# A sparse-attention and spectral-mixing kernel: its last two modes by column halves, the first output item's identity products moved, and four-mode weight transfers from an earlier pair on

## The chip, the cores and the metric

The kernel runs on one core of a Trainium2 chip. The metric is the device time in microseconds (us); the runs of the kernel before have a median of 425.84. The core has a matrix engine (PE, with its weight loads listed as PEld), a vector engine (DVE), an activation engine (ACT), a general engine (POOL) and a sync engine (SP). Sixteen DMA engines move data; POOL and SP issue the transfers here. PE writes its results into PSUM, which has 8 banks of 2 KB in each of 128 partitions; ACT and DVE read them from there.

## The reference

Attention over 8 batches, 8 heads, 576 positions and 64 channels, with a local mask for the first four heads and a strided one for the others; then a spectral layer over the 576 positions with 64 modes, each with its own complex 512 x 512 weight, and a residual product with `w_ch`.

```
scores = scale * np.matmul(q, k.transpose(0, 1, 3, 2))
mask_local = (rel >= 0) & (rel < stride)                    # heads 0 to 3, stride 32
mask_strided = (rel >= 0) & (pos[None, :] % stride == pos[:, None] % stride)
attn = softmax(np.where(masks, scores, -1e9));  x = np.matmul(attn, v)   # to (8, 576, 512)
X = np.fft.rfft(x, axis=1)[:, :n_modes]
Yr = np.einsum('bmd,mde->bme', Xr, w_r) - np.einsum('bmd,mde->bme', Xi, w_i)
Yi = np.einsum('bmd,mde->bme', Xr, w_i) + np.einsum('bmd,mde->bme', Xi, w_r)
y = np.fft.irfft(Yr + 1j * Yi, n=S, axis=1)
u = x + y
return u + np.maximum(u @ w_ch, 0.0)
```

The weights `w_r` and `w_i` are 64 x 512 x 512 in float32, 134 MB together; everything else is small beside them.

## The kernel before

**Weights.** A mode's weights are worked in two halves of the 512 input rows, so there are 128 half-modes, listed in `ORDER` (L150) in the order of their use. Two neighbours make a pair, 64 pairs in all. `w_fetch` (L161) issues the transfers from POOL, one for `w_r` and one for `w_i`, with a cast to float16. Most go into `wring`, a ring of five pair buffers; pairs 1, 2 and 7 (`GUEST`) go into tiles that are needed for something else later. `w_fetch` counts freed pair buffers; it issues the next transfer when there are enough: one for a pair, two if the pair's number is in `QUADS` (L153), in which case one transfer brings four half-modes (this pair and the next). The first eight pairs are fetched during the strided attention; after that each `mode_pair` (L589) calls `w_fetch` when its pair has been multiplied, unless that pair was in a guest tile. Three of the `w_r` transfers (those that begin at half-mode 64, 84 and 94) are cut by `UNEVEN` into pieces of uneven row counts (L187). The last four half-modes come one by one (L194). POOL also issues the loads of q, k and v (`load_str`, `load_loc`); `load_loc` for batch 6 is the last one before the local attention starts, and the one for batch 7 follows after the first 14 half-modes.

**Stages.** Strided attention, then local attention with the first 56 half-modes between its steps, then 48 half-modes of the other half with the "premix" products `x @ w_ch`, then the `rest` (L1061): 8 half-modes of slot 0 and 16 of slot 1, with the inverse transforms of the first 48 modes (`renew`) hung between them by the table `late`. All instructions stand in program order (`manual_schedule`): each engine works its own queue in that order and waits by semaphores.

**PSUM in the last stage.** A pool `p` with three double banks (`psum("p", pair=True)`) and a pool `y` with two banks. A new tile takes the next buffer of its pool in turn, and its first writer waits until the old tile's readers are done. Slot 0's modes and slot 1's first 48 go through `mode_pair`; slot 1's modes from 48 on are worked by `mode` (L618) itself: 16 products of 128 x 128 weights by 16 columns each, four per block `e` of 128 output channels; eight modes share one `y` tile. `spectrum` (L563) then moves finished modes to SBUF: DVE adds them to what slot 0 left, giving the tile `YT`. In the last group modes 56 to 61 are moved together and then 62 and 63 together (`ends`, L643).

**The end.** The 18 output items (`items`) are pairs of 128-row blocks. Item k has two sums, v and u, each in a double bank: `v_early` (L994) and `u_early` (L1002) start them with two identity products each; `new_rows` (L1009) adds the inverse transform of the last 16 modes, from `zzs` (for v) and `yys` (for u); `v_done` (L1036) is ACT's relu of v, `u_done` (L1048) is DVE's sum and SP's transfer to the output. `u_early` takes its buffer from `p` for even items and from `u` for odd ones. For the first four batches `zzs[0]` comes from `spec_z(3, 0, ...)` (four products with `w_ch`, L745) and `yys[0]`, `yys[1]` from eight transposes (L1076). Before the change these two steps use a pool of their own (`ps_s`) in the space of `y`, and `u` is opened in that space afterwards. The hook `late[22]` runs between modes 62 and 63.

Of the kernel before, what the change touches and what calls it, by code (L numbers as in the profile page):

```python
# [10 lines left out]
FP = mybir.dt.float32  # L11
F16 = mybir.dt.float16
# [7 lines left out]
NM = 64  # L20
# [36 lines left out]
def kernel(  # L57
# [10 lines left out]
    nc = tc.nc  # L68
    PSUM = bass.MemoryType.PSUM
# [5 lines left out]
    pss = {}  # L75
# [10 lines left out]
    def psum(kind, half=False, pair=False):  # L86
        if pair:
            return pss[kind].tile([128, 2, 512], FP, tag=kind, name=kind)
        if half:
            return pss[kind].tile([128, 1024], F16, tag=kind, name=kind)  # L90
        return pss[kind].tile([128, 512], FP, tag=kind, name=kind)
# [19 lines left out]
    idn = cs["cI"]  # L111
# [8 lines left out]
    YS = {}  # L120
# [29 lines left out]
    ORDER = [(1, m) for m in range(SPLIT1)] + [(0, m) for m in range(SPLIT0)]  # L150
    ORDER += [(1, m) for m in range(SPLIT1, NM)] + [(0, m) for m in range(SPLIT0, NM)]
    UNEVEN = {64: (25, 12, 27), 84: (6, 54, 4), 94: (10, 54)}
    QUADS = {p for p in range(13, 54) if (p - 13) % 5 in (0, 2)}  # L153
    wring = pw.tile([128, 2 * NWBUF, 4, DM], F16, tag="w", bufs=1, name="wring")
    w_tiles = []
    w_chs = {}
# [4 lines left out]
    def w_fetch(n=1):  # L161
        free_pairs[0] += n
        while len(w_tiles) < 2 * NM:
            i = len(w_tiles)
            pair = i // 2
            nm = 4 if pair in QUADS else 2
            if 2 * free_pairs[0] < nm:
# [86 lines left out]
    def act_copy(out, in_):  # L254
        nc.scalar.activation(out=out, in_=in_, func=ACTF.Copy)  # L255
# [300 lines left out]
    ypt = {}  # L556
    queued = []

    def flush():
        while queued:  # L560
            queued.pop()()

    def spectrum(slot, part, src):  # L563
        if slot == 0:
            nc.scalar.activation(out=YS["Y0"][part], in_=src, func=ACTF.Copy)
        else:
            nc.vector.tensor_tensor(
                out=YS["YT"][part], in0=src, in1=YS["Y0"][part], op=AluOp.add
            )
# [19 lines left out]
    def mode_pair(slot, m):  # L589
        half = 1 - slot  # L590
        if m % 4 == 0:
            ypt[slot] = psum("y")
        yp = ypt[slot]
        steps = [(c, mm) for c in range(4) for mm in (m, m + 1)]
        if m == 0:
            steps.sort(key=lambda x: x[1])
        for c, mm in steps:
            wt = w_tiles[ORDER.index((half, mm))]
            pr = ds(0, 128 if mm else 64)
            a = 32 * (mm % 4)  # L600
            nc.tensor.matmul(  # L601
                yp[ds(a, 32), :],
                Xh[half][pr, c].rearrange("p b r (h m) -> p (b r h) m", h=2)[
                    :, :, mm % 32
                ],
                wt[pr, XC[c], :],
                start=(c == 0),
                stop=(c == 3),
                tile_position=(0, a),
            )  # L610
        if slot or m // 2 not in GUEST:
            w_fetch()
        if m % 4:
            yr = big.tile([128, DM], F16, tag="yr", name="yr")
            act_copy(yr, yp)
            queued.append(lambda: four_turned(slot, m - 2, yr))

    def mode(slot, m):  # L618
        half = 1 - slot
        if m % 2:  # L620
            flush()
        if slot == 0 or m < SPLIT0:
            if m % 2:
                mode_pair(slot, m - 1)
            return
        mi, mg = m % 8, m // 8
        if mi == 0:
            ypt[slot] = psum("y")
        yp = ypt[slot]
        yv = yp.rearrange("p (m e x) -> p m e x", m=8, e=4)  # L630
        wt = w_tiles[ORDER.index((half, m))]
        for e in range(4):
            for c in range(4):
                nc.tensor.matmul(
                    yv[:, mi, e, :],
                    wt[:, XC[c], ds(128 * e, 128)],
                    Xh[half][:, c, :, :, m],
                    start=(c == 0),
                    stop=(c == 3),
                )  # L640
        if m % 2:
            w_fetch()
        ends = {5: 6, 7: 2} if mg == 7 else {7: 8}  # L643
        if mi in ends:
            n = ends[mi]
            m0 = mi + 1 - n
            spectrum(
                slot,
                (slice(None), slice(None), mg // 2, slice(None), ds(8 * (mg % 2) + m0, n)),
                yp.rearrange("p (m e x) -> p e x m", m=8, e=4)[:, :, :, ds(m0, n)],  # L650
            )
# [90 lines left out]
    def spec_z(g, bq, zp):  # L742
        for e in range(4):
            lhs = YS["YT"][:, e, g, ds(8 * bq, 8), :].rearrange("p x m -> p (x m)")
            nc.tensor.matmul(  # L745
                zp, lhs, w_chs["n"][:, e, :], start=(e == 0), stop=(e == 3)
            )
# [102 lines left out]
    for b in range(B):  # L850
# [3 lines left out]
        ends = [lambda h=h: loc_scores(b, h, True) for h in (0, 2)]  # L854
# [23 lines left out]
    zzs = [ptr.tile([128, DM], F16, name=f"zz{i}") for i in range(B)]  # L878
    yys = [ptr.tile([128, DM], F16, name=f"yy{i}") for i in range(B)]
# [22 lines left out]
    for b in range(B + 1):  # L902
        for t in range(5):
            if b > 0 and (t < 4 or b % 2 == 0):
                work.append(lambda b=b, t=t: premix(b - 1, t))
            if b < B and t < 4:
                half, cp = ((1, 0), (1, 1), (0, 0), (0, 1))[t]
# [68 lines left out]
    late = {0: [lambda: spec_late(spec_z, zzs, act_copy)], 1: [spec_last]}  # L976
    for n, i in enumerate([3, 5, 7] + list(range(8, 21))):
        b, t = n // 2, n % 2 * 2
# [15 lines left out]
    def v_early(k):  # L994
        vps[k] = psum("p", pair=True)
        for j, r in enumerate(own(items[k], v0s, v0h)):
            nc.tensor.matmul(vps[k][:, j], idn, r, start=True, stop=False)  # L997

    def pooled(k, j):
        return j == 1 and k in (4, 5, 6)  # L1000

    def u_early(k):  # L1002
        ups[k] = psum(("p", "u")[k % 2], pair=True)
        for j, r in enumerate(own(items[k], xos, xoh)):
            if pooled(k, j):
                continue
            nc.tensor.matmul(ups[k][:, j], idn, r, start=True, stop=False)
# [51 lines left out]

    flush()  # L1060
    rest = [(0, m) for m in range(SPLIT1, NM)] + [(1, m) for m in range(SPLIT0, NM)]  # L1061
    late[22] = [lambda: v_early(0), lambda: v_early(1), lambda: u_early(0)]
    for i, (slot, m) in enumerate(rest):
        mode(slot, m)
        for w in late.get(i, ()):
            w()
    yctx.close()
    with tc.tile_pool(name="ps_s", bufs=1, space=PSUM) as pss["s"]:
        zp = pss["s"].tile([128, 512], FP, name="zp")
        yp = pss["s"].tile([128, 2, 512], F16, name="yp")  # L1070
        spec_z(3, 0, zp)
        act_copy(zzs[0], zp)
        for bq in range(2):
            for e in range(4):
                lhs = YS["YT"][:, e, 3, ds(8 * bq, 8), :].rearrange("p x m -> p (x m)")
                nc.tensor.transpose(yp[:, bq, ds(128 * e, 128)], lhs, idn)  # L1076
        for bq in range(2):
            nc.vector.tensor_copy(out=yys[bq], in_=yp[:, bq])
    pss["u"] = pctx.enter_context(tc.tile_pool(name="ps_u", bufs=1, space=PSUM))

    for k in range(2):
# [1 line left out]
    for k in range(2):  # L1083
        v_done(k)
    for k in range(2):
        if k:
            u_early(k)
        new_rows(k, ups[k], yys)
        u_done(k)
    for k in range(2, LAST + 2):  # L1090
# [47 lines left out]
```

## Time and profile before

| | us |
|---|---|
| median of 3 runs (425.5 to 427.29) | 425.84 |
| profiled execution | 425.88 |
| its span, first to last instruction | 424.1 |
| PE busy | 340.9 (80%) |
| DVE busy | 234.6 (55%) |
| ACT busy | 219.0 (52%) |
| POOL busy | 95.7 (23%) |
| first output transfer issued (SP) | 395.42 |
| last output transfer issued (SP) | 419.1 |

A busy share is an average over the whole span, and the stages differ: what sets the time has to be read stage by stage. Matmuls overlap in the profile, so PE's share is not its share of peak. The granted clock of PE was 0.933 on average. The profile names an engine's idle time by what ended it ("<-DMA wring" is a wait for a weight transfer, "<-PE y" one for a product). The trace also stamps each transfer's completion once for each of the sixteen DMA engines; a reader of the data waits for the last of them.

The transfers by size, from the list of DMA issues: 17 of `w_r` and 16 of `w_i` have 1024 KB (four half-modes), 22 and 24 have 512 KB (pairs), and three of each in the guest tiles have 512 KB. The outputs are 14 transfers of 512 KB and 8 of 256 KB.

### The profile page before, as it was taken

How to read it: one execution, taken by the hardware profiler on the slowest of the kernel's cores; microseconds unless marked ns; L12 is line 12 of the kernel's file. 1: busy time of each engine (PE TensorE's matmuls, PEld its weight loads, DVE VectorE, ACT ScalarE, POOL GpSimd, SP SyncE). 2: the span in 40 equal slices, each digit the busy share in tenths (PEclk: the TensorE clock that was granted, in tenths of full speed). 3: DMA queues.
4: the chain of work that ended last, by engine and by line, in shares of the span. 5: the costliest groups of instructions: out<-in, count | busy, mean ns of one | idle time of the engine just before them, and what ended most of it. 6: DMA issues, size and time to landing. Idle time of an engine off the chain costs nothing.

```text
span 424.1 us, 9718 instructions
## 1 busy us (share of the span) xinstructions
PE 340.9 (80%) x4164; PEld 206.5 (49%) x4164; DVE 234.6 (55%) x469; ACT 219.0 (52%) x391; POOL 95.7 (23%) x165
## 2 busy tenths in 40 slices
PE   2987878769999298889874959895779979989993
PEld 2866767554656155556542425453344534535331
DVE  3788788950354134545323326864385646555794
ACT  1687678642666056565753323622162365534772
POOL 7332333322422011102122101212111232310200
PEclk9999899967999789999998789999798998989999
DMA  8999999999999999999999999999999999997598
GB/s 147 211 212 213 213 212 214 210 212 210 214 214 211 215 216 213 214 215 214 211 215 213 212 211 216 213 213 214 213 214 211 214 214 214 213 213 145 196 380 316
DMA packets 30347, 91.62 MB, mean 216 GB/s; under 512 B 3873, under 2 KB 4641, under 8 KB 30305
## 3 DMA queue, kind: packets, MB, share of 16 engines
q0 software_dynamic: 24624, 81.28, 96.7%
q1 hardware_dynamic: 5248, 9.65, 6.2%
q8 instruction: 32, 0.52, 0.5%
q10 hardware_dynamic: 432, 0.08, 0.1%
q14 instruction: 11, 0.08, 0.0%
HBM read 162.83 MB, written 9.44 MB: 406 GB/s over the span
## 4 chain that ended last, share of the span: by engine, by line
PE 46%; DMA 23%; DVE 17%; ACT 8%; issue 4%; POOL 1%; DVEq 0%; ACTq 0%; POOLq 0%
DMA wring<-in_moe_w_i_dram 22%; PE y L601 11%; PE sc L726 5%; DVE xb L245 3%; ACT X L255 3%; DVE kz L287 3%; DVE yy L761 2%; PE p L997 2%; PE tp L417 2%; PE y L536 2%; PE sc L536 2%; PE sc L463 2%; PE p L769 2%; PE p L1018 1%; ACT PL L493 1%
## 5 line engine op out<-in xcount | busy, mean ns | idle before, releaser
L601 PE MATMUL y<-wring,X 128*32 128x512 f16 (+1 forms) x424 | 65.8, 422 | 23.6 <-DMA wring<-in_moe_w_i_dram 23.6
L190 POOL DMA_DIRECT2D wring<-in_moe_w_r_dram x39 | 23.6, 606 | 204.3 <-PE y L601 180.6
L601 PEld LDWEIGHTS <-X 128*32 128x32 f16 (+1 forms) x448 | 27.5, 139 | 41.4 <-DMA wring<-in_moe_w_i_dram 24.3
L735 ACT ACTIVATE v<-sc 128x512 f16<-128x512 f32 x32 | 19.1, 597 | 45.4 <-PE sc L726 45.4
L736 DVE COPY xo<-tp 128x512 f16<-128x512 f16 x32 | 22.1, 691 | 36.5 <-PE tp L734 36.4
L255 ACT ACTIVATE yr<-y 128x512 f16<-128x512 f32 x28 | 16.7, 597 | 41.2 <-PE y L601 41.0
L726 PE MATMUL sc<-w_cp,xT 128*128 128x512 f16 x128 | 36.2, 404 | 1.9 <-DVE xT L694 1.9
L245 DVE TENSOR_TENSOR xb<-av,rec 90x256 f16<-90x256 f32 (+2 forms) x80 | 36.0, 450 | 2.8
L493 ACT ACTIVATE PL<-sc 128x480 f16<-128x480 f32 (+1 forms) x48 | 26.9, 578 | 20.1 <-PE sc L479 19.8
L244 DVE RECIPROCAL rec<-av 90x4 f32<-90x4 f32 (+2 forms) x80 | 14.6, 183 | 39.3 <-PE av L508 28.2
L424 DVE COPY qT<-tp 128x576 f16<-128x576 f16 x16 | 11.9, 752 | 38.1 <-PE tp L417 38.1
L971 DVE TENSOR_TENSOR xo<-p,xo 128x1024 f16<-128x1024 f32 x16 | 19.6, 1225 | 14.3 <-PE p L769 14.3
L190 POOL DMA_DIRECT2D wring<-in_moe_w_i_dram x42 | 25.6, 609 | 6.1 <-DMA ring<-in_k_dram 2.0
L382 ACT ACTIVATE PL<-sc 90x360 f16<-90x360 f32 (+1 forms) x48 | 22.7, 490 | 7.1 <-PE sc L375 6.6
L255 ACT ACTIVATE v<-p 128x1024 f16<-128x1024 f32 x16 | 16.4, 1024 | 17.4 <-PE p L769 17.4
L255 ACT ACTIVATE v<-tp 128x640 f16<-128x640 f16 (+1 forms) x24 | 19.0, 807 | 11.6 <-PE tp L451 9.3
L417 PE MATMUL tp<-cI_s,ring 64*64 64x64 f16 x864 | 22.2, 196 | 2.7 <-DVE qT L424 2.4
L463 PE MATMUL sc<-cMl_s,cI_s 128*128 128x480 f16 (+1 forms) x48 | 18.9, 395 | 5.1 <-ACT PL L493 3.5
L280 PE MATMUL tp<-cI_s,ring 72*128 72x72 f16 x256 | 15.4, 207 | 9.1 <-DMA ring<-in_v_dram 7.4
L255 ACT ACTIVATE kz<-tp 64x360 f16<-64x360 f16 (+1 forms) x32 | 18.9, 592 | 6.2 <-PE tp L417 5.2
L417 PEld LDWEIGHTS <-ring 64*64 64x64 f16 x864 | 17.3, 109 | 9.0 <-issue 4.9
L536 PEld LDWEIGHTS <-xb 108*128 108x128 f16 (+2 forms) x176 | 15.4, 106 | 11.7 <-DVE xb L245 7.6
(146 smaller groups left out, 747.9 us busy)
## 6 DMA issues: line engine op xcount, KB each, us to landing
wring<-in_moe_w_r_dram POOLq DMA_DIRECT2D x17, 1024.0 KB, 13.3
wring<-in_moe_w_i_dram POOLq DMA_DIRECT2D x16, 1024.0 KB, 17.5
wring<-in_moe_w_i_dram POOLq DMA_DIRECT2D x24, 512.0 KB, 15.1
wring<-in_moe_w_r_dram POOLq DMA_DIRECT2D x22, 512.0 KB, 13.4
out_dram<-osb SPq DMA_DIRECT2D x14, 512.0 KB, 3.8
ring<-in_v_dram POOLq DMA_DIRECT2D x8, 288.0 KB, 13.3
ring<-in_q_dram POOLq DMA_DIRECT2D x8, 288.0 KB, 13.5
ring<-in_k_dram POOLq DMA_DIRECT2D x8, 288.0 KB, 13.1
```

Of the source, the lines that this page charges most:

```text
L190: nc.gpsimd.dma_start(dst, rows)
L245: nc.vector.tensor_tensor(out=dst, in0=val.rearrange("p h (q c) -> p h c q", c=4), in1=rec[0:n, 0:pieces] .to_broadcast((n, pieces, 64)) . ...
L255: nc.scalar.activation(out=out, in_=in_, func=ACTF.Copy)
L382: nc.scalar.activation(out=PS[0:n, ds(POFF[t], 4 * n)], in_=scp[0:n, 0 : 4 * n], func=ACTF.Exp, scale=SCALE,)
L417: nc.tensor.transpose(tp[ds(64 * hp, 64), ds(64 * i, 64)], qn[ds(64 * hp, 64), ds(64 * (9 * g + i), 64)], idn[ds(64 * hp, 64), ds(64 * hp, ...
L463: nc.tensor.matmul(scp[:, 0 : n * times].rearrange("p (h x) -> p h x", h=times), idn, mask_rows("cMl", n, times), start=True, stop=False,)
L493: nc.scalar.activation(out=dst, in_=src, func=ACTF.Exp, scale=SCALE)
L536: nc.tensor.matmul(xp[:, ds(192 * cp, 192)].rearrange("p (f m) -> p f m", f=3), xb[b][0:n, base + t, ds(128 * cp, 128)], F[0:n, :, t, :], ...
L601: nc.tensor.matmul(yp[ds(a, 32), :], Xh[half][pr, c].rearrange("p b r (h m) -> p (b r h) m", h=2)[:, :, mm % 32], wt[pr, XC[c], :], start= ...
L726: nc.tensor.matmul(vp, xT[:, ch], w_chs["cp"][:, ch, :], start=(ch == 0), stop=(ch == 3),)
L736: nc.vector.tensor_copy(out=xo.rearrange("p (h q c) -> p h q c", h=2, c=4), in_=tp[:, 0:512].rearrange("p (h c q) -> p h q c", h=2, c=4),)
L971: nc.vector.tensor_tensor(out=xo, in0=up[:, 0:n], in1=xo, op=AluOp.add)
```

## The change

Three parts.

1. `QUADS` starts at pair 8 instead of 13, in the same rhythm: it gains the pairs 8 and 10, so that pairs 8 and 9 come by one transfer of `w_r` and one of `w_i`, and pairs 10 and 11 as well.
2. The last two modes (62 and 63 of slot 1) are written to two new `y` tiles, one for the blocks e = 0, 1 and one for e = 2, 3, instead of the group's tile. In mode 63 each half of both modes is moved by `spectrum` as soon as its two blocks are done.
3. Between modes 62 and 63 only item 1's v is started (two products). Item 0's v is started after the last `spec_z`, ahead of the transposes, and item 0's u just before its `new_rows`. The tiles for `spec_z` and the transposes are taken from `y`; the pool `ps_s` is gone, and `y` is closed after them.

```
-    QUADS = {p for p in range(13, 54) if (p - 13) % 5 in (0, 2)}
+    QUADS = {p for p in range(8, 54) if (p - 8) % 5 in (0, 2)}
...
+        if m == NM - 2:
+            ypt["last"] = [psum("y") for _ in range(2)]
+        if m >= NM - 2:
+            yl = [y.rearrange("p (m e x) -> p m e x", m=8, e=4) for y in ypt["last"]]
         wt = w_tiles[ORDER.index((half, m))]
         for e in range(4):
+            if m >= NM - 2:
+                yv = yl[e // 2]
             for c in range(4):
...
+            if m == NM - 1 and e % 2:
+                es = slice(e - 1, e + 1)
+                spectrum(
+                    slot,
+                    (slice(None), es, mg // 2, slice(None), ds(14, 2)),
+                    yv[:, ds(6, 2), es].rearrange("p m e x -> p e x m"),
+                )
...
-        ends = {5: 6, 7: 2} if mg == 7 else {7: 8}
+        ends = {5: 6} if mg == 7 else {7: 8}
...
-    late[22] = [lambda: v_early(0), lambda: v_early(1), lambda: u_early(0)]
+    late[22] = [lambda: v_early(1)]
     for i, (slot, m) in enumerate(rest):
         mode(slot, m)
         for w in late.get(i, ()):
             w()
+    zp = psum("y")
+    yp = psum("y", half=True).rearrange("p (b x) -> p b x", b=2)
+    spec_z(3, 0, zp)
+    act_copy(zzs[0], zp)
+    v_early(0)
+    for bq in range(2):
+        for e in range(4):
+            lhs = YS["YT"][:, e, 3, ds(8 * bq, 8), :].rearrange("p x m -> p (x m)")
+            nc.tensor.transpose(yp[:, bq, ds(128 * e, 128)], lhs, idn)
+    for bq in range(2):
+        nc.vector.tensor_copy(out=yys[bq], in_=yp[:, bq])
     yctx.close()
-    with tc.tile_pool(name="ps_s", bufs=1, space=PSUM) as pss["s"]:
-        zp = pss["s"].tile([128, 512], FP, name="zp")
-        yp = pss["s"].tile([128, 2, 512], F16, name="yp")
-        spec_z(3, 0, zp)
...
     for k in range(2):
-        if k:
-            u_early(k)
+        u_early(k)
         new_rows(k, ups[k], yys)
         u_done(k)
```

More of the change, by code (lines that the diff above doesn't have):

```diff
@@ L1066 @@
             w()
-    yctx.close()
-    with tc.tile_pool(name="ps_s", bufs=1, space=PSUM) as pss["s"]:
-        zp = pss["s"].tile([128, 512], FP, name="zp")
-        yp = pss["s"].tile([128, 2, 512], F16, name="yp")
-        spec_z(3, 0, zp)
[L1072 to L1078, printed above, removed]
+    zp = psum("y")
[9 more added lines that the diff above has]
+        nc.vector.tensor_copy(out=yys[bq], in_=yp[:, bq])
+    yctx.close()
     pss["u"] = pctx.enter_context(tc.tile_pool(name="ps_u", bufs=1, space=PSUM))
```

## The prediction, made before the change was run

> **What bounds the kernel now.** I read the page's 40 slices first, then the DMA queues, the timeline of POOL around the transfers that change, and the timeline and the chain of waits at the end.
>
> ```profile
> PEclk9999899967999789999998789999798998989999
> DMA  8999999999999999999999999999999999997598
> GB/s 147 211 212 213 213 212 214 210 212 210 214 214 211 215 216 213 214 215 214 211 215 213 212 211 216 213 213 214 213 214 211 214 214 214 213 213 145 196 380 316
> ...
> q0 software_dynamic: 24624, 81.28, 96.7%
> ```
>
> From slice 1 to slice 35 the DMA engines never rest: 210 to 216 GB/s, all from POOL's queue (q0). PE waits for it (the largest entry of the chain is the weights' DMA, 22%). So the time has two parts: when the last weight lands, and what follows. A stamp per DMA engine (sixteen per transfer) in the trace gives the last weight's landing: 388.39 on the first engine, 390.66 on the last, mean 389.39. Everything behind it is a tail of 424.1 - 390.66 = 33.4 us.
>
> POOL's rows where the first four-mode transfers will stand:
>
> ```profile
> 97.90 0.54 POOL L233 DMA_DIRECT2D ring<-in_k_dram  x1 [0.86 <-DMA ring<-in_v_dram]
> 101.10 0.60 POOL L190 DMA_DIRECT2D wring<-in_moe_w_r_dram  x1 [2.66 <-PE y L601]
> 101.70 0.60 POOL L190 DMA_DIRECT2D wring<-in_moe_w_i_dram  x1
> 107.70 0.58 POOL L190 DMA_DIRECT2D wring<-in_moe_w_r_dram  x1 [5.40 <-PE y L601]
> 108.27 0.60 POOL L190 DMA_DIRECT2D wring<-in_moe_w_i_dram  x1
> 110.31 0.59 POOL L190 DMA_DIRECT2D wring<-in_moe_w_r_dram  x1 [1.44 <-PE y L601]
> 110.88 0.60 POOL L190 DMA_DIRECT2D wring<-in_moe_w_i_dram  x1
> 112.25 0.59 POOL L190 DMA_DIRECT2D wring<-in_moe_w_r_dram  x1 [0.77 <-PE y L601]
> ```
>
> Columns: start, duration, engine, line, what, and the idle time before with its releaser. Pair 8 goes out at 101.10 when pair 0's buffer is free, pair 9 at 107.70 (pairs 1 and 2 sit in guest buffers and free nothing), 10 at 110.31, 11 at 112.25. POOL waited for PE, not for the queue, before each.
>
> **The change, part by part.**
>
> *Four-mode transfers from pair 8.* QUADS gains 8 and 10; all later members stay. A four-mode transfer needs two freed pairs, so pairs 8 and 9 go out together at 107.70 instead of 101.10 and 107.70; pairs 10 and 11 together at 112.25. What is left in the queue meanwhile? The last load before it is the one issued at 97.90. Its sixteen stamps run from 105.66 to 108.86, mean 107.03. In the kernel before, the 1 MB of 101.10 and 101.70 carried the queue over (4.9 us per engine); now nothing does. How long after its issue does a four-mode transfer begin to move? Three places where an engine had run dry show it: issues at 156.41, 241.78 and 316.98 had their first stamps at 164.17, 249.33 and 324.40; a four-mode transfer takes an engine 4.89 (steady step between stamps), so they began 2.86, 2.66 and 2.51 after the issue. I take 2.65: first bytes at 110.35. The engines idle 110.35 - 108.86 = 1.5 us (the last one) to 4.7 us (the first), on average 3.3 us. The nearest row for a shorter start is the program's first load, issued at 1.23 with its first packet at 2.91 (1.7 us): mean idle 2.35. Bounds 2.3 to 3.6.
>
> The Trainium skill's page "DMA: Bandwidth & Descriptors" (section Specifications) gives about 1 us to the first byte on the gpsimd path; counted from the end of the 0.6 us issue row this would put the first bytes at 109.3, the mean idle at 2.3 and the whole about 1 us earlier than my sum. The three rows above contradict it here, by some 1 us.
>
> The stream has no slack to win this back, except where engines run dry later in the kernel before: at 156.41, 241.78, 316.98 and 331.23 the mean stamp came 0.15, 0.20, 0.27 and 0.16 us later than its bytes explain. Engines that are late anyway do not wait there; I give back 0.6 (bounds 0 to 0.8). Four transfers fewer: a pair steps by 2.455, a four-mode transfer by 4.89, so a merge saves 0.02 per engine, 0.1 in all. Stream: +3.3 - 0.6 - 0.1 = **+2.6** on the mean stamp, and I move the last stamp with it: 390.66 to 393.3. For the last stamp alone the bounds are wider: +1.3 if the refill levels the engines so that all end near the new mean (389.39 + 2.6 = 392.0), +4.1 if those that idled 4.7 end last (4.7 - 0.6).
>
> What else the late issues touch: PE wants pair 8 at 120.89; the four-mode pair lands at about 110.35 + 2 x 4.89 = 120.1, level. Pairs 10 and 11 land at some 130, where PE took pair 10 at 128.27; PE falls back 2 us there, but it stands idle for 8.16 us before 147.66, waiting for pair 13. That cover is large, so nothing. POOL's later queue keeps its order; SP's has only the outputs.
>
> *The tail up to the first output.* PE's last weights, then the chain:
>
> ```profile
> 390.77 0.60 PEld L634 LDWEIGHTS <-wring 128*128 128x128 f16 x16 [0.25 <-issue]
> 391.52 0.29 DVE L567 TENSOR_TENSOR YT<-y,Y 128x128 f16<-128x128 f32 x1 [1.90 <-PE y L634]
> 391.87 1.04 PE L745 MATMUL zp<-w_ch,YT 128*128 128x512 f16 x4 [0.39 <-DVE YT L567]
> 392.53 0.65 PEld L1076 LDWEIGHTS <-YT 128*128 128x128 f16 x8
> 392.99 0.60 ACT L255 ACTIVATE zz<-zp 128x512 f16<-128x512 f32 x1 [4.03 <-PE zp L745]
> ```
>
> Mode 63 starts 0.11 after the landing (390.66): the six identity products (0.217 us apart, 1.3 us) ran in the wait for it. Taking four of them out of there therefore gains at most 0.08 (PE was free at 390.85). That mode 62 no longer waits for DVE (389.08) gains nothing for the same reason.
>
> Column halves: half one's addition on DVE starts after 8 of 16 products (0.24 of 0.49 us) and takes about 0.22 (128 columns 0.29, 384 columns 0.55: 0.16 + 0.001 each). So the first w_ch product can start at 391.55 instead of 391.87, the third at 391.98 when half two is in: **-0.3** for zz, or 0 if the product's wait covers both halves.
>
> Against it: v_early(0), two products, 0.43, now stands ahead of the eight transposes. Before, PE waited 0.29 for zz there (next L1018 at 393.64). Now PE comes to zz's products at 392.42 + 0.43 + 0.61 = 393.46, just behind zz (393.27): relu of item 0 starts 0.18 earlier. Then u_early(0), 0.43, stands between zz's and yy's products, so the first output addition is at about 394.8 instead of 394.70: **+0.1**.
>
> The costlier step is the rotation of the three "p" buffers. Before, the order of allocation is v(0), v(1), u(0), v(2): v(2) takes v(0)'s buffer, v(3) takes v(1)'s. The chain of waits shows both stalls:
>
> ```profile
> 394.09 1.07 ACT rl L1041 x2
> 395.16 0.04 issue
> 395.21 0.59 PE p L997 x2
> 395.80 0.32 PE p L1018 x2
> 396.12 0.01 issue
> 396.12 0.59 PE p L997 x2
> ```
>
> v(2) runs when item 0's two relu pieces are through (395.16), v(3) about when item 1's is (1.02 later). Now the order is v(1), v(0), u(0), v(2): v(2) takes v(1)'s buffer and waits for item 1's relu, at about 396.0. Behind it in PE's queue stand zz's products of item 2 (so ACT's next relu and DVE's next sum) and everything after. v(3) then runs at once. Rebuilt step by step: v(2) 396.0, zz 396.4, v(3) 396.65, u(2) 397.1, zz(3) and yy(2) 397.5, v(4) 397.9; before 397.47. From there PE sets the beat (16.00 busy of 16 us from 400 to 416), so **+0.45** on the end. Without the gain from the halves it is +0.8; at best, if DMA (376 GB/s, share 1.01) sets the end and only the first output counts, -0.2. I take +0.35, PE's free 0.08 included.
>
> **Sum.** Profiled execution 425.88 (span 424.1 and 1.8 around it) + 2.6 + 0.35 = **428.8**. The median of the runs, 425.84, is the same to 0.04. What a measurement of this kernel tells from no change is about 0.5%, 2.1 us (423.7 to 428.0).
>
> **The rivals.**
>
> *The refill levels the engines (0.20).* The spread of the stamps (105.66 to 108.86) is wiped out at 110.35, and the late engine, which ended last, idles only 1.5. For: the split transfers of line 187 change the order of the engines, so who is last is open. Against: the mean must still move 2.6. Then +1.3 + 0.35: 427.5, not slower by my bound. It decides if the last weight's last stamp is under 392.3.
>
> *The engines part further (0.17).* The splits at 221, 268 and 290 shift packets from engines that were behind; now the early ones have idled 4.7, the late ones 1.5, so the splits push the wrong way. +4.1 + 0.45: 430.4.
>
> *The queue doesn't run dry (0.07).* If PE reached pair 3 before 103, the 2.65 us would hide behind 105.66. Against: nothing ahead of 107.70 changes. Then the tail alone: between 425.88 - 0.2 and + 0.8, say 426.2.
>
> *Fewer transfers gain (0.02).* If each transfer held the queue for a fixed time, four fewer would pay. The shortest time from issue to landing of any output (2.1 us, tile osb) bounds such a price from above: 4 x 2.1 = 8.4, 417.5. The steady steps of 2.455 and 4.89 speak against it. The Trainium skill's page "DMA: Bandwidth & Descriptors" (section Anatomy of one DMA) puts a fixed part of about 2 us on each transfer and advises batching, though it calls most of it completion latency; the trace agrees that behind a full queue it isn't paid.
>
> **How the numbers follow.** The forecast has 0.54. Slower than 428.0: the forecast but for 0.04 of it (0.50), the parted engines (0.17), and the levelled ones where the tail takes its high bound (0.02): 0.69. Faster: 0.02, the fixed price. Same: the rest, 0.29. Range: low end from the levelled engines with the tail's best bound, 425.88 + 1.3 - 0.2 = 427.0, a little under it for the short start (426.8); high end 431, the parted engines with the tail's +0.8.
>
> **What would show it.** POOL's first four-mode issue near 107.7 and a hole in DMA share at 106 to 110; the last weight's landing near 393.3; 4 POOL transfers fewer; the third and fourth relu further from the second; v(2) behind item 1's relu. Wrong if DMA share stays above 1 through 105 to 112, or if the tail from landing to end is not 33.4 + 0.35.

## The result, and the profile after

The changed kernel takes 431.07 us (median of 6 runs, 428.94 to 433.13); the kernel before takes 425.82 beside it. The ratio is 1.0118, 95% interval 1.008 to 1.0157: slower by some 5 us. The profiled execution took 432.53 us, its span is 430.8, and it is the second longest of the six. A second profile, taken later in an execution of 430.79 us (experiment `after_again`), serves as a cross-check.

The page's 40 slices and its main queue, after:

```profile
PEclk9999899968998779999998889998798999998899
DMA  8999999999999999999999999999999999995498
GB/s 149 211 212 213 214 212 213 211 210 189 177 215 212 213 214 211 208 214 215 211 216 212 214 213 213 214 212 209 210 211 209 213 214 214 213 213 106 181 381 317
...
q0 software_dynamic: 24560, 81.28, 96.0%
```

Two slices now fall out of the flat row, 189 and 177 GB/s around 97 to 118 us. Later ones sit a little low (208 to 210), where the kernel before has 211 to 216. And the dip before the outputs is deeper (106 and 181, where it had 145 and 196). 64 packets fewer, for the same bytes, are the four merged transfers.

POOL's rows at the first place (start, duration, engine, line, what, idle time before and its releaser):

```profile
97.56 0.54 POOL L233 DMA_DIRECT2D ring<-in_k_dram  x1 [0.82 <-DMA ring<-in_v_dram]
107.51 0.63 POOL L190 DMA_DIRECT2D wring<-in_moe_w_r_dram  x1 [9.41 <-PE y L601]
108.13 0.63 POOL L190 DMA_DIRECT2D wring<-in_moe_w_i_dram  x1
112.06 0.61 POOL L190 DMA_DIRECT2D wring<-in_moe_w_r_dram  x1 [3.30 <-PE y L601]
112.66 0.62 POOL L190 DMA_DIRECT2D wring<-in_moe_w_i_dram  x1
```

The row of 101.10 is gone, and POOL waits 9.41 us for PE to free pair 3. The windows of the same kernel (length, busy time of the five engines, granted clock, DMA share, GB/s) show the queue running dry:

```profile
105.00:107.00 2.00, 2.00 (x25) 1.03 (x21) 0.69 (x2) 0.57 (x1) 0.00 (x0) 1.00 0.80 151
107.00:109.00 2.00, 1.99 (x49) 1.46 (x49) 1.20 (x2) 1.35 (x3) 1.25 (x2) 1.00 0.35 43
109.00:111.00 2.00, 2.00 (x35) 1.40 (x33) 1.05 (x4) 0.72 (x2) 0.00 (x0) 1.00 0.94 164
```

By the sixteen stamps of the first four-mode transfer (mean 115.01), less those of the load before it (107.03) and the usual step of 4.89, the mean engine lost 3.09 us here. The trace's packet records say how: the transfer is issued at 107.51, its first packet starts at 108.84, 1.33 us later, and the first sixteen packets take 0.49 to 0.93 us each, where 0.324 is usual. So the hole is empty time and then slow first packets. The last weight's stamps: mean 393.56, last 395.00, where they were 389.39 and 390.66. So the landing moved by 4.3 us, and the tail from the landing to the end grew from 33.4 to 35.8.

The tail, in the timeline of the changed kernel ("x16" is the number of instructions in the row):

```profile
392.61 0.64 PE L640 MATMUL y<-X,wring 128*128 128x16 f16 x16 [1.06 <-DMA wring<-in_moe_w_i_dram]
393.08 0.59 PE L1010 MATMUL p<-v,cI_s 128*128 128x512 f16 x2
395.13 0.64 PE L640 MATMUL y<-X,wring 128*128 128x16 f16 x16 [1.46 <-DMA wring<-in_moe_w_i_dram]
...
395.85 1.89 PE L758 MATMUL y<-w_ch,YT 128*128 128x512 f16 x4
...
397.54 1.06 PE L1010 MATMUL p<-v,cI_s 128*128 128x512 f16 x2
...
398.39 1.06 PE L1088 MATMUL y<-cI_s,YT 128*128 128x128 f16 x8
...
402.31 0.94 SPq L1071 DMA_DIRECT2D out_dram<-osb  x2
```

The four w_ch products take 1.89 us where they took 1.04, the identity pair 1.06 where it took 0.59, the eight transposes 1.06 where they took 0.61: PE runs at half speed. The windows (granted clock is the third number from the end) say the same:

```profile
394.00:396.00 2.00, 0.79 (x17) 0.69 (x18) 0.42 (x2) 0.00 (x0) 0.00 (x0) 0.67 0.02 4
396.00:398.00 2.00, 2.00 (x6) 0.65 (x5) 0.03 (x1) 0.22 (x1) 0.00 (x0) 0.50 0.00 0
398.00:400.00 2.00, 2.00 (x15) 1.09 (x14) 0.51 (x2) 0.38 (x1) 0.00 (x0) 0.50 0.00 0
```

The trace has the clock at 0.5 from 394.7 to 401.5. In the kernel before it is at 1.0 from 381.2 to 422.2.

### The profile page after: what moved, and what is told of

The parts are those of the page before. It is cut to its first block, busy times and chain, and to the rows that moved or that the text cites. A ratio compares the mean times of both kernels' runs of the same rounds, so it can differ in the third digit from the quotient of the medians.

```text
span 430.8 us, 9713 instructions
## 1 busy us (share of the span) xinstructions
PE 342.8 (80%) x4164; PEld 206.9 (48%) x4164; DVE 234.8 (55%) x470; ACT 219.2 (51%) x391; POOL 93.3 (22%) x161
## 4 chain that ended last, share of the span: by engine, by line
PE 39%; DMA 32%; DVE 16%; ACT 6%; issue 4%; POOL 1%; DVEq 0%; POOLq 0%; ACTq 0%
DMA wring<-in_moe_w_i_dram 31%; PE y L601 9%; PE sc L739 5%; DVE xb L245 3%; ACT X L255 3%; DVE kz L287 3%; DVE yy L774 2%; PE p L1010 2%; PE sc L536 2%; PE y L536 2%; PE tp L417 2%; PE sc L463 2%; PE p L1031 2%; ACT PL L493 1%; PE tp L747 1%
## 5 line engine op out<-in xcount | busy, mean ns | idle before, releaser
L190 POOL DMA_DIRECT2D wring<-in_moe_w_r_dram x37 | 22.5, 609 | 214.4 <-PE y L601 190.2
L244 DVE RECIPROCAL rec<-av 90x4 f32<-90x4 f32 (+2 forms) x80 | 14.6, 183 | 39.3 <-PE av L508 28.2
L190 POOL DMA_DIRECT2D wring<-in_moe_w_i_dram x40 | 24.4, 609 | 7.6 <-DMA wring<-in_moe_w_i_dram 3.5
L255 ACT ACTIVATE kz<-tp 64x360 f16<-64x360 f16 (+1 forms) x32 | 18.9, 592 | 6.2 <-PE tp L417 5.2
L1054 ACT ACTIVATE rl<-p 128x1024 f32<-128x1024 f32 (+1 forms) x19 | 18.4, 979 | 7.2 <-PE p L1031 5.3
```

Of the source, the lines that this page charges most:

```text
L190: nc.gpsimd.dma_start(dst, rows)
```

## The experiments

Twelve experiments ran, one of them the changed kernel again. Each bears on one of two parts of the time, the stream of weights or the tail behind its last landing. A table at the end of each part sets the profiles side by side.

### The stream

**`quads_only`**: the kernel before with the first part of the change alone.

```
-    QUADS = {p for p in range(13, 54) if (p - 13) % 5 in (0, 2)}
+    QUADS = {p for p in range(8, 54) if (p - 8) % 5 in (0, 2)}
```

> The kernel before with the wider QUADS alone. If the queue running dry at 107 sets the stream: DMA share falls to about 0.4 between 107 and 109, the last weight lands 4 to 4.5 us later than before (about 395.0), and the time is 429.5 to 430.5, as the six identity products still fill PE's wait for mode 63. If the tail alone made the kernel slower: 425.8.

Measured: 429.77, ratio 1.008 (1.0059 to 1.0101). The hole is there (3.31 us) and the last landing is at 393.98. This part makes up some two thirds of the loss. (The profiled execution, the longest of the six, lost another 2 us between the last landing and mode 63; `tail_fill` below comes back to that.)

**`hole_only`**: the kernel before; pair 8 is to be issued only when two pairs are free.

```
-            if 2 * free_pairs[0] < nm:
+            if 2 * free_pairs[0] < (4 if pair == 8 else nm):
```

> The kernel before, QUADS from 13, but pair 8 is held back until pair 3 is free too, so that pairs 8 and 9 go out together as pairs: the same hole in the queue with no new four-mode transfer. If the hole and the engines starting in step behind it cost: last landing +4 to 4.5, as quads_only, 429.5 to 430.5, and packets above 330 ns in many places. If the hole costs only its own 3 us and four-mode transfers are slower by themselves: +2.6, 428.5. If four-mode transfers are all of it: 425.8.

Measured: 426.11, ratio 1.0011 (0.9998 to 1.0024), and no hole. POOL's rows in this kernel say why:

```profile
97.10 0.54 POOL L233 DMA_DIRECT2D ring<-in_k_dram  x1 [0.83 <-DMA ring<-in_v_dram]
100.79 0.60 POOL L190 DMA_DIRECT2D wring<-in_moe_w_r_dram  x1 [3.15 <-PE y L601]
101.39 0.60 POOL L190 DMA_DIRECT2D wring<-in_moe_w_i_dram  x1
107.50 0.58 POOL L190 DMA_DIRECT2D wring<-in_moe_w_r_dram  x1 [5.52 <-PE y L601]
```

Pair 8 still goes out at 100.79. Its place in the program moved, but POOL waits only for the buffer's last reader, and that is pair 0. The experiment did not make what it was meant to make; it says only that the place in the program is not what holds an issue back.

**`quad10_only`**: the kernel before with one more four-mode transfer, where there is no dry queue.

```
-    QUADS = {p for p in range(13, 54) if (p - 13) % 5 in (0, 2)}
+    QUADS = {p for p in range(13, 54) if (p - 13) % 5 in (0, 2)} | {10}
```

> The kernel before with pair 10 added to QUADS and not 8: one more four-mode transfer of each kind, issued at 112.25 while the queue still holds 10 us of work, so no hole. If the hole is the cause: 425.8, last landing 390.7. If a four-mode transfer is slower by itself (step 5.05 for 4.89): +0.3, 426.2.

Measured: 426.06, ratio 1.0009 (0.9994 to 1.0023), last landing 390.00. A four-mode transfer shows no cost from being large, and no gain from being one fewer.

**`hole2`**: a hole without any new four-mode transfer. Pair 8 takes pair 3's buffer and so really waits for it.

```
-            if 2 * free_pairs[0] < nm:
+            if 2 * free_pairs[0] < (4 if pair == 8 else nm):
...
                 a = 2 * ((pair - sum(g < pair for g in GUEST)) % NWBUF)
+                a = {8: 2, 9: 0}.get(pair, a)
```

> The kernel before, its four-mode transfers from pair 13 as they were; pair 8 is held until two pairs are free and takes pair 3's buffer, pair 9 takes pair 0's. So both go out near 107.5, as two-mode transfers, and the engines run dry near 107 to 110 as in the changed kernel. Theory (the hole, and the engines that start again in step and then slow one another): a hole of 3.1 to 3.3 us on the mean engine, then packets of 4096 bytes longer than 330 ns in more than 4% of the cases up to 235 us, last landing 393.5 to 395, time 429 to 430 like that of the kernel with the four-mode transfers alone (429.8). Rival A (it is the row of four-mode transfers after the hole that makes the packets longer): the hole stays, the packets do not get longer, last landing near 393, time near 428.3. Rival B (the hole is won back at later dry places): last landing under 392, time under 427.5.

Measured: 429.3, ratio 1.007 (1.0051 to 1.009), last landing 394.66. POOL's rows:

```profile
97.33 0.54 POOL L234 DMA_DIRECT2D ring<-in_k_dram  x1 [0.87 <-DMA ring<-in_v_dram]
107.67 0.60 POOL L191 DMA_DIRECT2D wring<-in_moe_w_r_dram  x1 [9.80 <-PE y L602]
...
108.85 0.60 POOL L191 DMA_DIRECT2D wring<-in_moe_w_r_dram  x1
```

The hole is 3.52 us here, with ordinary pairs behind it, and the kernel loses about as much as `quads_only`. So it is the late issue that costs, not the size of the transfers. Rivals A and B both fall: the landing is 1.7 and 2.7 us later than they said.

But the landing (mean stamp +4.28) moved by more than the hole. The rest sits in the packets. A packet of 4096 bytes usually takes 324 ns in all of these traces; after the hole a part of them takes longer, most of these 340 to 390. Two windows of the changed kernel:

```profile
289.00:291.00 2.00, 2.00 (x20) 1.00 (x17) 0.81 (x3) 1.10 (x2) 1.21 (x2) 1.00 1.12 197
291.00:293.00 2.00, 1.98 (x19) 1.12 (x20) 1.84 (x5) 0.69 (x2) 0.01 (x1) 1.00 1.06 203
```

and the same two of the kernel before:

```profile
289.00:291.00 2.00, 2.00 (x17) 0.98 (x16) 0.81 (x2) 0.17 (x1) 0.64 (x2) 1.00 1.07 215
291.00:293.00 2.00, 1.61 (x19) 0.96 (x16) 1.70 (x4) 1.17 (x2) 1.24 (x2) 1.00 1.07 215
```

The engines are as busy (share 1.12 and 1.06) and move less (197 and 203 GB/s, not 215). Such a stretch is not idle time; the share alone would not show it.

**`after_even` and `before_even`**: the two kernels without the split transfers, to see whether the splits push the engines apart and whether engines that are far apart slow one another.

```
-    UNEVEN = {64: (25, 12, 27), 84: (6, 54, 4), 94: (10, 54)}
+    UNEVEN = {}
```

> The changed kernel without the three split transfers (modes' loads 64, 84 and 94 go out whole). In the changed kernel the stamps of the sixteen engines lie 6.3 us apart from 290 to 310, and 44% of the packets there take longer than 330 ns; in the kernel before 4.9 us and 0.3%. Theory (the splits push the engines the wrong way after the hole, and engines further apart than some 5.5 us lengthen one another's packets): spread under 5.5 us and under 10% long packets from 285 to 310, last landing 1 to 1.5 us earlier than 395.0, time about 429.8. Rival 1 (the long packets have nothing to do with the spread): a share of over 20% there again. Rival 2 (the splits level the engines even so): the spread grows beyond 6.5 us, the last landing is later, 432 or more.

> The kernel before without the three split transfers. Theory (spread lengthens packets, and the splits hold the spread down here): the spread from 290 to 310 goes beyond 5.5 us, over 10% of the packets there take longer than 330 ns against 0.3%, the last landing is 1 to 3 us later than 390.7, time 427 to 429. Rival (packets lengthen for another reason, bound to the hole): the spread grows but the packets keep 324 ns, and the last landing is later only by what the engines differ, under 1.5 us.

Measured: `after_even` 431.33, ratio 1.0102 (1.0067 to 1.0138), no different from the change with its splits. Its profiled execution was the shortest of the six by 3.4 us (427.65). There the first four-mode transfer went out at 106.75, the hole was only 2.07 us, the spread from 290 to 310 was 3.1 us and no packets were long; what the five longer runs did wasn't profiled, so the theory isn't decided by it. `before_even`: 426.85, ratio 1.0009 (0.999 to 1.0028). The spread stayed at 4.9 us and the packets at 324 ns, so what it was to test did not arise.

What the profiles show of the stream. "Hole" is how much later the first weight transfer after 97.9 us lands, on the mean of sixteen stamps, than its usual step explains. "Long packets" is the time beyond 324 ns of all packets of 4096 bytes from 109 us on, over sixteen engines. The last two columns are the stretch from 290 to 310 us: the mean distance of the first from the last stamp of a transfer, and the share of packets over 330 ns.

| kernel | first issue | hole | long packets | last weight, mean stamp | spread | long |
|---|---|---|---|---|---|---|
| before | 101.10 | 0.03 | 0.65 | 389.39 | 4.9 | 0.3% |
| hole_only | 100.79 | 0.21 | 1.40 | 390.24 | 6.3 | 5.7% |
| quad10_only | 101.09 | 0.02 | 0.69 | 389.16 | 4.8 | 0.5% |
| tail_fill | 100.41 | 0.15 | 2.19 | 390.67 | 6.7 | 30.7% |
| after_even | 106.75 | 2.07 | 0.51 | 390.81 | 3.1 | 0.2% |
| quads_only | 107.69 | 3.31 | 3.07 | 393.32 | 6.5 | 29.9% |
| hole2 | 107.67 | 3.52 | 2.93 | 393.67 | 5.7 | 39.9% |
| after | 107.51 | 3.09 | 3.60 | 393.56 | 6.3 | 44.0% |
| after_again | 107.93 | 3.87 | 2.14 | 393.34 | 5.8 | 18.9% |
| after_fill | 108.03 | 3.64 | 2.34 | 393.41 | 6.2 | 18.6% |

Read downwards, the hole follows the issue time. The four other profiles (`tail_only`, `order_swap`, `halves_only`, `before_even`) have holes of 0.02 to 0.3 us and 0.2 to 4.9% long packets from 290 to 310. All the stream's losses together (hole, long packets, later dry places; the last mean stamp less the steady steps of all transfers) come to some 2.0 us before and to some 6.2 in `after`, `after_again` and `after_fill`. So the rest, without hole and long packets, is 2.0 - 0.03 - 0.65 = 1.3 before, and 6.2 - 3.09 - 3.60 = -0.5, 0.2 and 0.2 after (below nothing, since a few long packets lie in the hole itself and count twice). By this estimate between 1 and 2 us of the hole are won back, and the long packets eat them up again.

Why packets lengthen stays open. The theory of `hole2`, that engines which start in step slow one another, does not hold as it stands: in `after` they are closest from 110 to 130 (1.3 us) with 8% long packets, and 44% are long at 290 to 310, where they are furthest apart. A spread over 5.6 us goes with more than 18% long packets in six of seven profiles, but it may be their consequence, and in `tail_fill` both came without a hole.

### The tail

**`tail_only`**: everything of the change but the transfers.

```
-    QUADS = {p for p in range(8, 54) if (p - 8) % 5 in (0, 2)}
+    QUADS = {p for p in range(13, 54) if (p - 13) % 5 in (0, 2)}
```

(against the changed kernel)

> The changed kernel with QUADS as before (from 13). The last weight should land at 390.7 as before. If PE's idle time before mode 63 costs its clock (granted clock 0.5 from there on), the tail from that landing to the end is about 35.5 instead of 33.4 and the time 427.5 to 428.2. If only the buffer rotation costs: clock 1.0, tail +0.35, time 426.2. If the moved products pay: 425.5 or less.

Measured: 428.01, ratio 1.0048 (1.0031 to 1.0064). The profiled execution, at 426.75, is one of the two short ones of six; its clock is at 1.0 through the tail. So no profile shows what the four longer executions lost.

**`order_swap`**: the kernel before with the order of allocation of the "p" buffers as in the change.

```
-    late[22] = [lambda: v_early(0), lambda: v_early(1), lambda: u_early(0)]
+    late[22] = [lambda: v_early(1), lambda: v_early(0), lambda: u_early(0)]
```

> The kernel before with item 1's identity products allocated ahead of item 0's, so that v(2) takes item 1's buffer as in the changed kernel. The prediction's step: v(2) waits for item 1's relu, about 0.8 us later, the end +0.45 to +0.8, 426.5 to 426.9. Rival (the outputs' transfers set the end, and later output additions hide behind them): 426.1, no difference, though v(2) starts later in the profile.

Measured: 425.7, ratio 0.9995 (0.9982 to 1.0007). Its chain of waits (start, length, what):

```profile
395.37 1.07 ACT rl L1041 x2
396.44 0.04 issue
396.48 0.59 PE p L997 x2
```

v(2) follows item 0's two relu pieces at 0.04 us, as before; item 1's relu, 1.02 us, only begins there. So v(2) still takes item 0's buffer: the one that the program frees first, not the one that it allocated first. The "next buffer of its pool in turn" in the description of the kernel before is not right for this pool. Nothing waits longer.

**`halves_only`**: the kernel before with the column halves; the six identity products stay between modes 62 and 63. The edit is the change's own, but for

```
-    late[22] = [lambda: v_early(1)]
+    late[22] = [lambda: v_early(0), lambda: v_early(1), lambda: u_early(0)]
...
     act_copy(zzs[0], zp)
-    v_early(0)
...
-        u_early(k)
+        if k:
+            u_early(k)
```

and the transfers from pair 13.

> The kernel before with the column halves of the last two modes alone; the six identity products stand between modes 62 and 63 as before and the buffers rotate as before. The prediction's step: the first w_ch product 0.32 us earlier after mode 63, -0.3 on the end, 425.7 to 425.8. Rival 1 (the product waits for both halves, or TensorE is late anyway): 426.0, no difference. Rival 2 (the split itself costs, since two additions of DVE take longer than one): +0.3, 426.4.

Measured: 425.66, ratio 0.9995 (0.9981 to 1.0008). The chain of waits:

```profile
390.46 0.41 PE y L640 x8
390.87 0.02 issue
390.89 0.24 DVE YT L567
391.13 0.05 issue
391.18 1.05 PE y L758 x4
```

The product starts after eight of the sixteen products and one short addition, 0.72 us after mode 63 begins; it was 1.02 (391.87 - 390.85). The profile shows the step, 0.36 us on the first output (4.21 instead of 4.57 us after mode 63 begins); it is too small for the runs to tell.

**`tail_fill` and `after_fill`**: `tail_only` and the changed kernel, with four more identity products in the wait for mode 63, so that six stand there as in the kernel before.

```
-    late[22] = [lambda: v_early(1)]
+    def fill(k):
+        vps[k] = psum("p", pair=True)
+        for j, r in enumerate(2 * own(items[k], v0s, v0h)):
+            nc.tensor.matmul(vps[k][:, j % 2], idn, r, start=True, stop=True)
+        for j, r in enumerate(own(items[k], v0s, v0h)):
+            nc.tensor.matmul(vps[k][:, j], idn, r, start=True, stop=False)
+
+    late[22] = [lambda: fill(1)]
```

> The tail of the changed kernel with the transfers of the kernel before, and four more identity products, which write item 1's buffer twice before its real ones, so that again six products stand between mode 62 and mode 63. Nothing of the result hangs on the four. Theory (the clock falls because TensorE stands idle in the wait for mode 63): the granted clock stays at 1.00 from 388 to 410 in the profile, and the time is 426.0 to 426.7, against 428.0 without the fill. Rival (the tail of the changed kernel is slow because its identity products and the buffer order stand in the path): the time stays at 427.7 to 428.5, or is longer, with the first output as late after the landing as without the fill.

> The changed kernel with four more identity products between modes 62 and 63, which write item 1's buffer twice before its real ones; nothing of the result hangs on them. Theory (in the wait for mode 63 TensorE stands idle, the granted clock falls, and the tail grows by some 2.2 to 2.6 us): no half clock in the 10 us behind the landing, the first output some 4.6 us after mode 63 begins instead of 7.2, and the ratio falls by what the fill took off the tail alone (1.0048 to 1.0005), to about 1.0075, 429.3. Rival (the transfers alone make the kernel slow, and the clock in the profile was one run's chance): 430.5 to 431.1, as without the fill.

Measured: `tail_fill` 426.36, ratio 1.0005 (0.9984 to 1.0027), against 1.0048 (from 1.0031 on) without the fill: more work made it faster, as the theory said. That the half clock is what the fill took away is not shown by these two, since neither profile has it in the tail; that is left to the profiles of `after_fill` and `after_again` below. Two of the twelve runs took 429.1 and 429.2, and the profile fell on the latter. There the loss came earlier. Three windows:

```profile
376.00:380.00 4.00, 2.93 (x22) 1.31 (x23) 0.68 (x1) 0.63 (x2) 1.03 (x2) 0.61 1.06 213
380.00:384.00 4.00, 4.00 (x27) 1.34 (x26) 1.92 (x2) 1.10 (x3) 0.52 (x1) 0.50 1.06 212
384.00:388.00 4.00, 4.00 (x41) 2.01 (x40) 1.70 (x2) 1.99 (x2) 0.00 (x0) 0.61 1.06 212
```

PE idled 1.65 us in a wait for weights up to 377.07, the clock fell at 376.8, and PE then worked without rest at half speed and came to mode 63 only 2.93 us after its weights had landed. `quads_only` shows the same, 2.01 us late after an idle time of 1.86 us up to 379.96 and a half clock from 379.5 to 386.4; so does `before_even`, 2.05 us late, with 2.01 us up to 377.19 and a half clock from 376.9 to 383.8. This loss ahead of the tail comes with and without the change. So the expected full clock from 388 on held, and the time of that one execution was still lost to the clock.

`after_fill`: 430.09, ratio 1.0084 (1.0051 to 1.0118). The profile:

```profile
392.48 1.02 PE L1078 MATMUL p<-v,cI_s 128*128 128x512 f16 x4
...
393.34 0.59 PE L1080 MATMUL p<-v,cI_s 128*128 128x512 f16 x2
...
394.48 0.64 PE L640 MATMUL y<-X,wring 128*128 128x16 f16 x16 [0.55 <-DMA wring<-in_moe_w_i_dram]
...
395.20 1.04 PE L758 MATMUL y<-w_ch,YT 128*128 128x512 f16 x4
...
399.12 0.94 SPq L1071 DMA_DIRECT2D out_dram<-osb  x2
```

PE idles 0.55 us instead of 1.46, the w_ch products take 1.04 again, and the first output goes out 4.64 us after mode 63 begins. The profile says what the theory said; the intervals of the ratio with and without the fill overlap, so on the time of the whole change the fill's gain is not shown.

**`after_again`**: the changed kernel once more.

> The changed kernel itself in another execution, to see which of its parts hold from run to run. Hole: 3.0 to 3.6 us on the mean engine, since nothing ahead of 107 depends on chance. Last landing 393.5 to 395 by packets that lengthen somewhere between 110 and 320 us, not at the same place. Tail: if TensorE idles over 1 us in the wait for mode 63, the half clock and 35.5 to 36 us from landing to end; if it idles under 0.7 us, full clock and some 33.2 us. If the half clock comes without such an idle time, or the idle time without the half clock, the account of the tail is wrong.

Measured: 430.71, ratio 1.0106 (1.0087 to 1.0125). Hole 3.87, somewhat above the expected range; last landing 394.34. The tail:

```profile
394.48 0.64 PE L640 MATMUL y<-X,wring 128*128 128x16 f16 x16 [1.39 <-DMA wring<-in_moe_w_i_dram]
395.19 1.04 PE L758 MATMUL y<-w_ch,YT 128*128 128x512 f16 x4
396.07 0.74 PE L1010 MATMUL p<-v,cI_s 128*128 128x512 f16 x2
396.60 1.06 PE L1088 MATMUL y<-cI_s,YT 128*128 128x128 f16 x8
```

The idle time of 1.39 us is there, and so is the half clock, but from 396.4 to 399.8: later and half as long, so the tail is 34.7 us and not the 35.5 to 36 expected.

The length of one idle time does not decide alone. In the same trace PE waited longer for weights at two earlier places, and the clock stayed at 1.00:

```profile
350.36 1.08 PE L601 MATMUL y<-wring,X 128*32 128x512 f16 x8 [1.71 <-DMA wring<-in_moe_w_i_dram]
359.87 0.65 PE L640 MATMUL y<-X,wring 128*128 128x16 f16 x16 [1.55 <-DMA wring<-in_moe_w_i_dram]
350.00:354.00 4.00, 3.62 (x26) 1.83 (x26) 3.90 (x7) 3.73 (x7) 1.18 (x2) 1.00 1.06 213
360.00:364.00 4.00, 3.87 (x50) 2.11 (x48) 1.82 (x2) 1.97 (x3) 0.67 (x2) 1.00 1.06 214
```

`after_even` has 1.70 and 1.95 us there, also without a fall. So the account of the tail stands on this. In five profiles the last weights land late (after 392) and PE is there in time. The two that idle 1.39 and 1.46 us ahead of mode 63 have the half clock; the three that idle 0.30 to 0.62 (`hole2`, `after_fill`, `after_even`) do not. The closest pair is `after_again` and `after_fill`: in both PE waits some 0.7 us ahead of mode 62 and mode 63 begins at 394.48, and only the wait between them differs, 1.39 us or 0.55. What else it takes stays open.

What the profiles show of the tail:

| kernel | last landing | to mode 63 | to first output | to the end | half clock in the tail |
|---|---|---|---|---|---|
| before | 390.66 | 0.19 | 4.57 | 28.7 | none |
| order_swap | 391.99 | 0.13 | 4.57 | 28.3 | none |
| hole2 | 394.66 | 0.13 | 4.58 | 28.3 | none |
| halves_only | 390.32 | 0.14 | 4.21 | 28.8 | none |
| quads_only | 393.98 | 2.01 | 4.57 | 28.7 | none |
| tail_only | 391.26 | 0.68 | 4.61 | 28.5 | none |
| tail_fill | 391.42 | 2.93 | 4.64 | 28.4 | none |
| before_even | 391.26 | 2.05 | 4.57 | 28.8 | none |
| after_fill | 394.35 | 0.13 | 4.64 | 28.5 | none |
| after_even | 392.74 | 0.13 | 4.64 | 28.4 | none |
| after_again | 394.34 | 0.14 | 6.05 | 28.5 | 3.4 us |
| after | 395.00 | 0.13 | 7.18 | 28.5 | 6.8 us |

From the first output on, everything takes 28.3 to 28.8 us whatever came before (28.2 and 28.7 in `hole_only` and `quad10_only`). What happens between landing and first output moves the end by just as much.

## Why the prediction was right, and where it was not

The direction was right, and for the reason given: the late issue makes a hole in the weight stream, and the hole moves the last landing. The time lies at the very top of the range: 431.07 and, in the later execution, 430.71, for a high end of 431.0. The forecast of 428.8 was too low by some 2 us, because its sum had nothing for two things: packets that lengthen, and the clock.

**The hole: right in size, not in its make-up.** Foreseen 3.3 us on the mean engine (bounds 2.3 to 3.6); measured 3.09 and 3.87 in the two profiles of the change, 3.5 and 3.6 in `hole2` and `after_fill`. The 2.65 us from issue to first bytes did not hold: the first packet starts 1.33 and 1.35 us after the issue in the two profiles (1.36 in `hole2`). The 2.65 was counted back from first stamps with packets at their usual length, so it held the slow first packets as well; that is why the sum came out. The page "DMA: Bandwidth & Descriptors" of the Trainium skill (section Specifications) gives about 1 us to the first byte, which the packets' 1.33 us does not contradict, although the prediction read it so; but the hole of 2.3 us worked out from it is too short here, since it leaves the slow first packets out.

**"I give back 0.6": the right kind of thing, but not the whole account.** By the estimate above the late engines won back more (1 to 2 us). But the sum assumed that a packet costs the same as before, and it does not: the long packets cost 2.1 and 3.6 us instead of 0.65. That is the first term that failed. The mean stamp moved 4.0 to 4.2 us instead of 2.6.

**"Taking four of them out of there therefore gains at most 0.08": the second step that failed.** It read the identity products in the wait for mode 63 as work that costs nothing either way. In the kernel before PE did not idle there. With two products, and with weights that land 4 us later, it idles 1.4 us; the clock falls to half in both profiles of the change, and products on the path take up to twice as long: the four w_ch products, the identity pair and the transposes in `after`, the transposes and what follows in `after_again`. Price 1.4 us in one profile, 2.5 in the other, where the step had nothing. By the prediction's own sign of being wrong, a tail other than 33.4 + 0.35, its account of the tail failed: 35.8 and 34.7. The Trainium skill's page "TensorE: Matmul & The Clock Gate" (section HAM oscillation — how this bites in real kernels) has as its rule "no PE-idle gaps >~3.4µs". Here half the clock followed idle times of 1.39 and 1.46 us, so the rule is too mild for this kernel; that the half clock comes in stretches of 3.4 and 6.8 us agrees with the window of about 3.4 us that the same page gives (Part 1: The HAM clock gate (the "warmup" mystery)).

**Column halves -0.3: right**, 0.36 by the profile. **The moved identity products +0.1: too low.** Both pairs stand on the path, and together they cost 4.61 - 4.21 = 0.40, which cancels the halves. **The rotation +0.45: wrong.** v(2) takes the buffer that comes free first; it costs nothing (`order_swap`). And since 28.2 to 28.8 us follow the first output in any case, a later v(3) would not have counted as foreseen. The sum of the three is +0.04 at full clock, for a forecast of +0.35: one term too high, one too low, and neither shows in the result beside the clock.

**The rivals.** The levelled engines (427.5): the refill did level them, to a spread of 1.3 and 1.8 us where it was 3.2, but the last stamp moved as far as the mean. The parted engines (430.4) come nearest in time, by another way: the last stamp lies 1.0 to 1.4 us behind the mean, before 1.27. So it is luck that the range reached to 431: its high end came from this rival, not from long packets or the clock. The queue that stays full is refuted by the windows at 107. Fewer transfers gain: `quad10_only`, no difference.

**Adding up**, in the profile nearest to the median (`after_again`, span 429.0 against 424.1):

| step | us |
|---|---|
| last landing | +3.68 |
| landing to mode 63 | -0.05 |
| mode 63 to first output (half clock 1.41 of it) | +1.48 |
| outputs | -0.2 |
| sum | +4.9 |

The landing follows the mean stamp (+3.95), which is made of the hole (+3.84), long packets (+1.49), other dry places (-1.1, by difference), the load ahead of the hole, 0.2 earlier, and four merges, 0.1.

No version here beats the kernel before beyond what a measurement can tell; `halves_only` is the only part of the change that its profile favours.

## What to carry to other kernels

A larger transfer needs more buffers free before it can go out; look at what is still in the queue at that moment, since a fully used stream has little to pay a hole back with (here 1 to 2 us of 3 to 4, by estimate). Work that stands in a wait on PE may not be free to remove: in two profiles without it the granted clock fell, and what came next on the path paid. Where the time after some event is the same in every profile (28.2 to 28.8 us behind the first output here), cost an edit by that event alone.

## What was not expected of the hardware

Packets of one size, 324 ns in an undisturbed stream, take mostly 340 to 390 ns in bursts of some 20 us after the queue has run dry (up to 44% of them from 290 to 310 us, at 197 to 203 GB/s instead of 215); in one profile of eight without a hole as well. The cause is open.

The first packet after the queue has run dry starts 1.32 to 1.36 us after the issue in all six profiles with a hole, and packets come slowly at first (0.49 to 0.93 us in `after`).

Late in the stream an idle time of 1.39 to 2.17 us on PE was often followed by half the clock, for 3.4, 6.8 or 10.2 us: in the tail of `after` from 0.4 us before the idle time ended, in that of `after_again` from 1.9 us after, and ahead of the tail in `before`, `tail_only`, `quads_only`, `tail_fill`, `before_even` and `after_even`. But idle times of 1.51 to 1.95 us in `after_again`, `after_even` and `quad10_only` left it at 1.0, and so did those of 0.3 to 0.65 us ahead of mode 63 (`after_even`, `after_fill`, `halves_only`, `hole2`). What decides is open.
